# Reordering the opening of a fused attention and gMLP kernel: all x chunks ahead of the first weights, next x chunks behind all weights, and 1/std spread by small stationary products

## The chip, the cores and the metric

The kernel runs on one core of a Trainium2 chip. The metric is the device time of one launch in microseconds; lower is better. A "span" is the length of the profiled part of one run. It is 2.0 to 2.1 us less than the time of that run for the kernel before. Before the change the time was 796.73 us (median of 3 runs, 796.6 to 797.34). Three later sessions, on chips that the record numbers 0 (experiments 1 to 4), 6 (5 to 8) and 5 (9 to 12), each with its own runs of the kernel before, gave medians of 796.76, 797.1 and 796.79 us.

## The reference, cut to what matters

```python
x = A_x                                            # [1, 2048, 1024], bf16
h  = x + A(layernorm(x), wq, wk, wv, wo, beta)     # 4 segments of 512 tokens, 32 heads of 32:
                                                   # causal attention within the segment, mixed by a gate
                                                   # sigmoid(beta) with a linear memory of earlier segments
h2 = h + B(layernorm(h), w_in, w_sp, b_sp, w_out)  # gelu, spatial matmul [2048 x 2048], w_out
```

Only the opening matters here: the normalization of the first 512 tokens (segment 0, four chunks of 128 tokens), its projections q, k and v, and the first steps of attention. A step is one group of four heads; there are 32 of them.

## The kernel before

A recorder notes every operation and inserts the semaphores that its operands need; each engine gets its own list, and in the timelines below its instructions come in that order. All operations carry the line of that recorder (L209) in the profile, so groups are told apart by their tiles.

In segment 0 the division by the standard deviation is put off: only the mean is taken off x before the projections, and 1/std multiplies v, q and k when they are evicted from PSUM. For q and k, 1/std must lie along the columns, so it is spread over all partitions (tile `rb`) by TensorE. The loads, all on one queue:

```python
for k in range(8):                       # order: x0, x1, wv0, x2, wv1, x3, wv2, wv3
    if k in (0, 1, 3, 5): x_load((k + 1) // 2)             # 128 rows of x, 256 KB
    else: ... sp.dma_start(WV[0][:, i:i + 2, :], ...)      # a quarter of w_v's first half, 256 KB
sp.dma_start(WK[:, :, 0:256], ...)
sp.dma_start(BETAB[:], ...)
sp.dma_start(WQ[:, :, 0:256], ...)
sp.dma_start(WV[1][:], ...)
```

The opening:

```python
warm(9)                                  # nine dummy products, stationary IDENT
act_mean(1)                              # ScalarE: mean of chunk 1
var0(ln_stats(XCH[0]))                   # VectorE: bn_stats x2, bn_aggr of chunk 0
c0 = center(0, MV[0][:, 0:1], ALU.subtract)
c1 = center(1, MEAN[1][:])
pe_Th(0, c0, dve, dve)                   # 8 transposes on TensorE, evicted by VectorE
pe_Th(1, c1, act, dve)
...                                      # 8 v products, chunk 2, 8 v products, chunk 3 (cut)
proj_v(0, 2, 0)
gates()                                  # sigmoid(beta): ScalarE, then three ops on VectorE
mask_g()                                 # GpSimd: copy of GS (1024 columns), four multiplies
mm8(bank(bk), ... WK ...)                # k of step 0
for i in range(2): pe.matmul(bank(br), ONES[:], DIAG[i] ...)     # spread 1/std
act.activation(RB[:], bank(br), ACTF.Copy)
qk_out(0, 1, bk)                         # VectorE: evict k times RB
mm8(bank(bq), ... WQ ...)
qk_out(0, 0, bq)
for tc in range(4, 8): x_load(tc)        # segment 1
sp.dma_start(WK[:, :, 256:D], ...)       # the rests of w_k and w_q, 1.5 MB each
sp.dma_start(WQ[:, :, 256:D], ...)
phi_exp(0); phi_max(0)                   # phi_max starts with a bf16 add of 1.0 on VectorE (tile pqk)
```

In step 0, the k product of step 1 fills PSUM bank 6, and the q product of step 1 is later written to the same bank. The program lets TensorE start that q product only when VectorE has evicted the k product (`qk_out`).

The softmax here doesn't subtract the row's maximum and nothing guards it: scores larger than these inputs give would overflow.

## Time and profile before

| | before |
|---|---|
| time, median | 796.73 us |
| TensorE busy | 789.9 of 795.1 us |
| first transpose | 6.10 us |
| first w_k product | 14.04 us |
| first logits (step 0) | 19.75 us |

The page of the kernel before: the first line is each engine's busy time, the second the chain of work that ended last, as shares of the span. PE is TensorE, PEld its loading of stationary operands, DVE is VectorE, ACT ScalarE, POOL GpSimd, and SPq the queue of SyncE, which issues the loads.

```profile
PE 789.9 (99%) x5657; PEld 378.4 (48%) x5657; DVE 379.3 (48%) x745; ACT 295.6 (37%) x347; POOL 172.1 (22%) x329
...
PE 96%; DMA 2%; DVE 1%; ACT 0%; SPq 0%; issue 0%
```

TensorE is all there is to gain from, and it is nearly full. So the next view is TensorE's timeline in the opening: start in us, duration in us, engine, line, operation, out<-in, shapes, count, and in brackets the idle time before the group and what ended it. Among the tiles, `lno` is a chunk with its mean taken off, `xnT` its transpose, `qk` the evicted q and k, and `e` the exponentials of the logits.

```profile
1.74 4.02 PE L209 MATMUL ps<-etmp,ident 128*128 128x512 bf16 x9 [1.74 <-DVE ident L209]
6.10 1.14 PE L209 MATMUL ps<-ident,lno 128*128 128x128 bf16 x16 [0.34 <-DVE lno L209]
7.09 0.39 PE L209 MATMUL ps<-wv,xnT 128*128 128x512 bf16 x1
7.71 1.68 PE L209 MATMUL ps<-wv,xnT 128*128 128x512 bf16 x7 [0.23 <-ACT xnT L209]
...
14.04 1.89 PE L209 MATMUL ps<-xnT,wk 128*128 128x512 bf16 x8
15.76 0.59 PE L209 MATMUL ps<-diag,ones 128*128 128x512 bf16 x2
...
19.75 0.40 PE L209 MATMUL ps<-qk 32*128 32x512 bf16 x4
...
21.81 0.59 PE L209 MATMUL ps<-xnT,wq 128*128 128x512 bf16 x2
...
24.72 0.29 PE L209 MATMUL ps<-qk 32*128 32x256 bf16 x4 [0.15 <-ACT e L209]
```

A product of 512 columns shows as 0.38 us, but eight of them start 0.216 us apart (14.04 to 15.76), so their records overlap. Read starts, not durations: from 6.10 on the starts follow each other almost without holes. What lies before 6.10, plus a few tenths at 7.31, 9.22, 24.4 and 29.8, is all that a better opening can give; the prediction estimates it at about 2 us.

### The profile page before, as it was taken

The page shows a single profiled execution, that of the slowest core. Times are in us where ns is not written, and L with a number is a line of the kernel's source. Part 1 is how long each engine was busy: PE and PEld are TensorE (multiplying, and loading weights), DVE is VectorE, ACT ScalarE, POOL GpSimd, SP SyncE. Part 2 cuts the span into 40 slices and gives each one's busy share as a digit, 9 for nine tenths or more (in the row PEclk, how much of TensorE's full clock was granted, in tenths as well). Part 3 has the DMA queues.
Part 4 walks back from the last instruction along what each step waited for, and adds up shares of the span by engine and source line. Part 5 has one row for each costly group of instructions (what it writes and reads, how often), then busy time and mean ns, then how long its engine had stood idle before and what let it go on. Part 6 is the DMA issues. An engine that isn't in the chain of part 4 may idle for free.

```text
span 795.1 us, 13111 instructions
## 1 busy us (share of the span) xinstructions
PE 789.9 (99%) x5657; PEld 378.4 (48%) x5657; DVE 379.3 (48%) x745; ACT 295.6 (37%) x347; POOL 172.1 (22%) x329
## 2 busy tenths in 40 slices
PE   8999999999999999999999999999999999999998
PEld 3445455554554455455544444444444444444444
DVE  7664689679854766744562000053234323323332
ACT  5777877887787675133333333100000000000000
POOL 4564565565553331100230000000000000000000
DMA  9862555363415325411116000740270043011002
GB/s 292 181 162 57 94 81 121 87 105 84 107 23 125 114 67 139 121 47 54 54 54 132 1 1 0 222 90 7 79 133 1 33 109 78 1 59 54 1 7 86
DMA packets 125002, 64.83 MB, mean 82 GB/s; under 512 B 94992, under 2 KB 113936, under 8 KB 124944
## 3 DMA queue, kind: packets, MB, share of 16 engines
q1 hardware_dynamic: 124944, 63.99, 33.7%
q8 instruction: 44, 0.72, 0.4%
q14 instruction: 14, 0.11, 0.1%
HBM read 32.51 MB, written 8.39 MB: 51 GB/s over the span
## 4 chain that ended last, share of the span: by engine, by line
PE 96%; DMA 2%; DVE 1%; ACT 0%; SPq 0%; issue 0%
PE ps L209 96%; DMA wq<-in_A_wq_dram 2%; DMA xch<-in_A_x_dram 0%; DVE stats L209 0%; ACT junk L209 0%; DVE xnT L209 0%; DVE lno L209 0%; SPq L209 0%; ACT xnT L209 0%; DVE mv L209 0%; DVE fin L209 0%
## 5 line engine op out<-in xcount | busy, mean ns | idle before, releaser
L209 PE MATMUL ps<-wspT,z 128*128 128x512 bf16 x896 | 194.0, 379 | 0.0
L209 ACT ACTIVATE e<-ps 128x2048 bf16<-128x2048 f32 (+1 forms) x96 | 152.6, 1590 | 41.9 <-PE ps L209 41.8
L209 PEld LDWEIGHTS ps<-wspT,z 128*128 128x128 bf16 x896 | 87.7, 98 | 105.7
L209 DVE TENSOR_TENSOR tmpg<-ps,brow 128x512 f32<-128x512 f32 x56 | 38.7, 691 | 196.7 <-DMA brow<-in_B_b_sp_dram 104.0
L209 POOL TENSOR_SCALAR_AFFINE_SELECT e<-e 128x512 bf16<-128x512 bf16 x128 | 90.4, 718 | 127.2 <-ACT e L209 127.1
L209 PE MATMUL ps<-win,hnT 128*128 128x448 bf16 x512 | 98.3, 352 | 0.0
L209 PE MATMUL ps<-w_out,yT 128*128 128x512 bf16 (+2 forms) x462 | 97.4, 373 | 0.0
L209 PE MATMUL ps<-hnT,win 128*128 128x512 bf16 x448 | 96.9, 379 | 0.0
L209 PEld LDWEIGHTS ps<-win,hnT 128*128 128x128 bf16 x512 | 49.7, 98 | 46.4 <-issue 0.2
L209 PEld LDWEIGHTS ps<-w_out,yT 128*128 128x128 bf16 x462 | 44.7, 98 | 52.3
L209 PEld LDWEIGHTS ps<-hnT,win 128*128 128x128 bf16 x448 | 43.8, 98 | 52.8
L209 PE MATMUL ps<-xnT,wk 128*128 128x512 bf16 x256 | 60.8, 380 | 0.0
L209 PE MATMUL ps<-xnT,wq 128*128 128x512 bf16 x256 | 60.6, 379 | 0.1
L209 PE MATMUL ps<-wv,xnT 128*128 128x512 bf16 x256 | 59.4, 380 | 0.2 <-ACT xnT L209 0.2
L209 ACT ACTIVATE z<-ps 128x448 bf16<-128x448 f32 x60 | 32.5, 543 | 69.4 <-PE ps L209 69.4
L209 PE MATMUL ps<-wo,oT 128*128 128x512 bf16 x256 | 58.0, 379 | 0.0
L209 ACT ACTIVATE z1T<-ps 128x512 bf16<-128x512 f32 x56 | 33.4, 597 | 63.3 <-PE ps L209 63.3
L209 DVE TENSOR_TENSOR fin<-fin,ps 128x512 bf16<-128x512 bf16 (+2 forms) x33 | 22.2, 671 | 71.2 <-DMA fin<-out_dram 39.7
L209 DVE BATCH_NORM_STATS2 zst<-z 128x6 f32<-128x448 bf16 x64 | 38.9, 619 | 30.1 <-ACT z L209 30.1
L209 PEld LDWEIGHTS ps<-v,e 128*128 128x128 bf16 x1280 | 38.8, 96 | 14.0 <-issue 6.5
L209 PE MATMUL ps<-v,e 128*128 128x33 bf16 x1280 | 42.2, 178 | 0.0
L209 DVE TENSOR_TENSOR yT<-tmpg,z1T 128x512 bf16<-128x512 f32 x56 | 38.8, 692 | 1.9
(86 smaller groups left out, 609.3 us busy)
## 6 DMA issues: line engine op xcount, KB each, us to landing
xch<-in_A_x_dram SPq DMA_DIRECT2D x16, 256.0 KB, 3.3
xr<-in_A_x_dram SPq DMA_DIRECT2D x16, 256.0 KB, 3.7
out_dram<-hch SPq DMA_DIRECT2D x16, 256.0 KB, 2.4
fin<-out_dram SPq DMA_DIRECT2D x16, 256.0 KB, 2.8
out_dram<-fin SPq DMA_DIRECT2D x31, 128.0 KB, 1.7
win<-in_B_w_in_dram SPq DMA_DIRECT2D x4, 896.0 KB, 5.1
w_out<-in_B_w_out_dram SPq DMA_DIRECT2D x1, 3584.0 KB, 12.7
win<-in_B_w_in_dram SPq DMA_DIRECT2D x3, 1024.0 KB, 5.2
```

Source lines behind the costliest of these rows:

```text
L209: ins = getattr(e, op.name)(*op.args, **op.kw)
```

## The change

The intent is to start real work earlier and to take work off VectorE. All four x chunks go ahead of w_v. Chunk 0's mean is taken in halves by two engines. Variances are computed later. The 512-column products with `DIAG` become eight 128-column products whose stationary operand is a broadcast column of 1/std. The rests of w_k and w_q go ahead of segment 1's x chunks, whose normalization starts two steps later. Smaller shifts that go with this, in which engine evicts some v products and in the order within steps 0 to 2, are cut.

```diff
-    for k in range(8): ...                      # x0 x1 wv0 x2 wv1 x3 wv2 wv3
+    for tc in range(4):
+        x_load(tc)
+    for i in range(0, 8, 2):
+        sp.dma_start(WV[0][:, i:i + 2, :], ...)
 ...
     sp.dma_start(WV[1][:], wcols(A_wv, 512, D))
+    sp.dma_start(WK[:, :, 256:D], wcols(A_wk, 256, D))      # moved up
+    sp.dma_start(WQ[:, :, 256:D], wcols(A_wq, 256, D))
 ...
-            pe.matmul(bank(7), IDENT[:], ETMP[:, 0, :], start=True, stop=True)      # warm
+            pe.matmul(bank(7), ETMP[:, 0, 0:128], ETMP[:, 0, :], start=True, stop=True)
 ...
     warm(9)
+    act_half(0)                    # ScalarE sums columns 512..1023
+    dve_half(0)                    # VectorE sums columns 0..511, adds the two
+    center_half(0, 0)
+    center_half(0, 1)
+    pe_Th(0, LNO[0], dve, dve)
+    act_mean(1)
+    v_pair(0, 0, 2)                # first two v products: need the first w_v piece
+    c1 = center(1, MEAN[1][:])
+    pe_Th(1, c1, dve, dve)
+    v_pair(0, 2, 4)
 ...                                # chunks 2 and 3 between the other v products
+    stats0(0, 0) ... stats0(3, 1)  # variances of chunks 0 and 3 on VectorE, 1 and 2 on ScalarE
+    dve.tensor_copy(RSB[:, 0, :], RSW[:, :, 0])             # 1/std as two bf16 parts
+    dve.tensor_tensor(RSB[:, 1, :], RSW[:, :, 0], RSB[:, 0, :], ALU.subtract)
     proj_v(0, 2, 0)
     mm8(bank(bk), ... WK ...)
+    q_part(0, bq, 0, 4)
+    for t in range(4):
+        for h in range(2):
+            pe.matmul(PS[:, br, t * 128:(t + 1) * 128], RSB[:, h, t:t + 1].to_broadcast([128, 128]), IDENT[:], ...)
     act.activation(RB[:], bank(br), ACTF.Copy)
     qk_out(0, 1, bk)
+    q_part(0, bq, 4, 8)
     qk_out(0, 0, bq)
+    gates()                        # moved behind the q/k evictions
+    mask_g()
 ...
-            f2 = [("qmm", n + 1, bq, 2, 8), ("qout", n + 1, 0, bq), ("vmm", 0, 0, 1, bv, 0, 2)]
+            f2 = [("qmm", n + 1, bq, 2, 8), ("qout", n + 1, 0, bq), ("vmm", 0, 0, 1, bv, 0, 3)]
```

More of the change, by code (lines that the diff above doesn't have):

```diff
@@ L321, in bass_sequential_preLN__memory_aug_infini_attn__mixer_gmlp__prompt_kernel @@
     RDM = cb("rdm", [128, 4, 4], F32)
-    RS0 = [cb("rs0%d" % i, [128, 1], F32) for i in range(4)]
+    RSW = cb("rsw", [128, 4, 8], F32)
+    RS0 = [RSW[:, i, 0:1] for i in range(4)]
     HNT = [tens("hnT0", [128, 8, L], BF16, 14 * K), tens("hnT1", [128, 8, L], BF16, 22 * K),
@@ L338, in bass_sequential_preLN__memory_aug_infini_attn__mixer_gmlp__prompt_kernel @@
     b1 = Bump(110 * K, 120 * K)
-    ONES = b1("ones", [128, 128], BF16)
+    HSUM = b1("hsum", [128, 1], F32)
     MEAN = [b1("mean%d" % i, [128, 1], F32) for i in range(4)]
     RB = b1("rb", [128, L], F32)
-    DIAG = [b1("diag%d" % i, [128, 4, 128], BF16) for i in range(2)]
+    RSB = b1("rsb", [128, 2, 4], BF16)
     JUNK = b1("junk", [128, D], BF16)
@@ L398, in wcols @@
         return ap[:, lo:hi].rearrange("(c p) n -> p c n", p=128)
-    for k in range(8):
-        if k in (0, 1, 3, 5):
-            x_load((k + 1) // 2)
-        else:
-            i = {2: 0, 4: 2, 6: 4, 7: 6}[k]
-            sp.dma_start(WV[0][:, i:i + 2, :],
-                         A_wv[i * 128:(i + 2) * 128, 0:512].rearrange("(c p) n -> p c n", p=128))
+    for tc in range(4):
+        x_load(tc)
+    for i in range(0, 8, 2):
+        sp.dma_start(WV[0][:, i:i + 2, :], A_wv[i * 128:(i + 2) * 128, 0:512].rearrange("(c p) n -> p c n", p=128))
     sp.dma_start(WK[:, :, 0:256], wcols(A_wk, 0, 256))
@@ L410, in bass_sequential_preLN__memory_aug_infini_attn__mixer_gmlp__prompt_kernel @@
     sp.dma_start(WV[1][:], wcols(A_wv, 512, D))
+    sp.dma_start(WK[:, :, 256:D], wcols(A_wk, 256, D))
+    sp.dma_start(WQ[:, :, 256:D], wcols(A_wq, 256, D))
     pool.memset(MHALF[:], -0.5)
-    dve.memset(ETMP[:], 0.0)
+    dve.memset(ETMP[:, 0, :], 0.0)
     act.activation(RDM[:, 0, 0:1], MHALF[:], ACTF.Exp)
@@ L418, in bass_sequential_preLN__memory_aug_infini_attn__mixer_gmlp__prompt_kernel @@
     pool.memset(BLK[:], 1.0)
-    pool.memset(ONES[:], 1.0)
     pool.affine_select(out=BLK[:], in_=BLK[:], pattern=[[-32, 4]], compare_op=ALU.is_ge, fill=0.0, base=0,
@@ L482, in v_out @@
         v = bank(b).rearrange("p (h d) -> p h d", d=32)
-        if (s, tcl, half) == (0, 3, 0):
-            dve.tensor_single_scalar(o, v, RS0[tcl][:], ALU.mult)
+        if (s, tcl, half) in ((0, 3, 0), (0, 0, 1)):
+            dve.tensor_single_scalar(o, v, RS0[tcl], ALU.mult)
         else:
-            act.activation(o, v, ACTF.Copy, scale=RS0[tcl][:] if s == 0 else 1.0)
+            act.activation(o, v, ACTF.Copy, scale=RS0[tcl] if s == 0 else 1.0)
     def v_mm(s, tcl, half, b, i):
@@ L681, in rstd0, with act_half @@
     def rstd0(tc):
-        pool.tensor_tensor(RS0[tc][:], RS[tc][:, 0:1], MHALF[:], ALU.pow)
-    def diag(tc):
-        dve.tensor_single_scalar(DIAG[0][:, tc, :], IDENT[:], RS0[tc][:], ALU.mult)
-        dve.scalar_tensor_tensor(DIAG[1][:, tc, :], IDENT[:], RS0[tc][:], DIAG[0][:, tc, :], ALU.mult, ALU.subtract)
+        pool.tensor_tensor(RS0[tc], RS[tc][:, 0:1], MHALF[:], ALU.pow)
     def pe_Th(tcl, src, e0, e1):
         pe_T(XNT[0], tcl, src, (e0, e1))
-    warm(9)
+    def act_half(tc):
+        act.activation(JUNK[:, 512:D], XCH[tc][:, 512:D], ACTF.Copy, scale=-1.0 / D, accum_out=MEAN[tc][:])
@@ new lines, in dve_half, with center_half, stats0 @@
+    def dve_half(tc):
+        dve.tensor_reduce(out=HSUM[:], in_=XCH[tc][:, 0:512], axis=mybir.AxisListType.X, op=ALU.add)
+        dve.scalar_tensor_tensor(MEAN[tc][:], HSUM[:], -1.0 / D, MEAN[tc][:], ALU.mult, ALU.add)
+    def center_half(tc, h):
+        dve.tensor_single_scalar(LNO[tc % 3][:, h * 512:(h + 1) * 512], XCH[tc][:, h * 512:(h + 1) * 512],
+                                 MEAN[tc][:], ALU.add)
+    def stats0(k, i):
+        dve.bn_stats(STATS[k][:, i, :], XCH[k][:, i * 512:(i + 1) * 512])
@@ L692, in bass_sequential_preLN__memory_aug_infini_attn__mixer_gmlp__prompt_kernel, with aggr0, v_pair @@
+    def aggr0(k):
+        dve.bn_aggr(MV[k][:], STATS[k][:])
+        var0(k)
+        rstd0(k)
+    def v_pair(t, lo, hi):
+        for i in range(lo, hi):
+            v_mm(0, t, 0, vb[t], i)
+    warm(9)
+    act_half(0)
[3 more added lines that the diff above has]
+    pe_Th(0, LNO[0], dve, dve)
     act_mean(1)
-    var0(ln_stats(XCH[0]))
-    c0 = center(0, MV[0][:, 0:1], ALU.subtract)
+    vb = [next_bank() for _ in range(2)]
+    v_pair(0, 0, 2)
     c1 = center(1, MEAN[1][:])
-    pe_Th(0, c0, dve, dve)
@@ L697, in bass_sequential_preLN__memory_aug_infini_attn__mixer_gmlp__prompt_kernel @@
-    pe_Th(1, c1, act, dve)
+    pe_Th(1, c1, dve, dve)
+    v_pair(0, 2, 4)
     act_mean(2)
-    rstd0(0)
-    var0(ln_stats(XCH[1]))
-    rstd0(1)
+    v_pair(1, 0, 4)
+    v_pair(0, 4, 6)
     c2 = center(2, MEAN[2][:])
     act_mean(3)
-    vb = [next_bank() for _ in range(2)]
-    for i in range(4):
-        for t in range(2):
-            v_mm(0, t, 0, vb[t], i)
-    pe_Th(2, c2, act, dve)
-    c3 = center(3, MEAN[3][:])
-    for i in range(4, 8):
-        for t in range(2):
-            v_mm(0, t, 0, vb[t], i)
@@ L713, in bass_sequential_preLN__memory_aug_infini_attn__mixer_gmlp__prompt_kernel @@
-    var0(ln_stats(XCH[2]))
-    rstd0(2)
-    pe_Th(3, c3, act, dve)
-    act_var(3)
-    rstd0(3)
-    diag(0)
-    v_out(0, 0, 0, vb[0])
-    diag(1)
-    diag(2)
-    diag(3)
-    v_out(0, 1, 0, vb[1])
-    proj_v(0, 2, 0)
+    pe_Th(2, c2, dve, act)
+    v_pair(1, 4, 6)
+    v_pair(0, 6, 8)
+    v_pair(1, 6, 8)
+    c3 = center(3, MEAN[3][:])
+    stats0(0, 0)
+    act_var(1)
+    rstd0(1)
+    pe_Th(3, c3, dve, act)
+    stats0(0, 1)
+    aggr0(0)
+    act_var(2)
+    rstd0(2)
+    stats0(3, 0)
@@ new lines, in bass_sequential_preLN__memory_aug_infini_attn__mixer_gmlp__prompt_kernel @@
+    stats0(3, 1)
+    aggr0(3)
+    dve.tensor_copy(RSB[:, 0, :], RSW[:, :, 0])
+    dve.tensor_tensor(RSB[:, 1, :], RSW[:, :, 0], RSB[:, 0, :], ALU.subtract)
+    rot["n"] = 4
+    proj_v(0, 2, 0)
+    v_out(0, 1, 0, vb[1])
+    v_out(0, 0, 0, vb[0])
+    bq, br, bk = 5, 6, 7
+    mm8(bank(bk), lambda i: WK[:, i, 0:128], lambda i: XNT[0][:, i, :])
+    q_part(0, bq, 0, 4)
+    for t in range(4):
+        for h in range(2):
+            pe.matmul(PS[:, br, t * 128:(t + 1) * 128], RSB[:, h, t:t + 1].to_broadcast([128, 128]), IDENT[:],
+                      start=(h == 0), stop=(h == 1))
@@ L725, in bass_sequential_preLN__memory_aug_infini_attn__mixer_gmlp__prompt_kernel @@
+    act.activation(RB[:], bank(br), ACTF.Copy)
+    qk_out(0, 1, bk)
+    q_part(0, bq, 4, 8)
+    qk_out(0, 0, bq)
     gates()
     mask_g()
-    bk, bq, br = next_bank(), next_bank(), next_bank()
-    mm8(bank(bk), lambda i: WK[:, i, 0:128], lambda i: XNT[0][:, i, :])
-    for i in range(2):
-        pe.matmul(bank(br), ONES[:], DIAG[i][:].rearrange("p c n -> p (c n)"), start=(i == 0), stop=(i == 1))
-    act.activation(RB[:], bank(br), ACTF.Copy)
-    qk_out(0, 1, bk)
-    mm8(bank(bq), lambda i: WQ[:, i, 0:128], lambda i: XNT[0][:, i, :])
@@ L734, in bass_sequential_preLN__memory_aug_infini_attn__mixer_gmlp__prompt_kernel @@
-    qk_out(0, 0, bq)
     for tc in range(4, 8):
         x_load(tc)
-    sp.dma_start(WK[:, :, 256:D], wcols(A_wk, 256, D))
-    sp.dma_start(WQ[:, :, 256:D], wcols(A_wq, 256, D))
     phi_exp(0)
@@ L741, in bass_sequential_preLN__memory_aug_infini_attn__mixer_gmlp__prompt_kernel @@
     rot["banks"] = [6, 7]
+    rot["n"] = 0
     CH = [("z2", FH + 448 * k, 448) for k in range(4)] + [("z1", 512 * k, min(512, FH - 512 * k)) for k in range(4)]
@@ L808, in fill @@
                  "vmm": v_part, "vout": v_out}[u[0]](*u[1:])
-        if s < NSEG - 1 and c < 4:
-            ln_tasks(XCH[c], XNT[(s + 1) % 2], c)
+        if s < NSEG - 1 and 0 <= c - 2 * (s == 0) < 4:
+            t = c - 2 * (s == 0)
+            ln_tasks(XCH[t], XNT[(s + 1) % 2], t)
         if s < NSEG - 2 and c >= 4:
@@ L817, in bass_sequential_preLN__memory_aug_infini_attn__mixer_gmlp__prompt_kernel @@
         if n == 0:
-            fill(f1)
-            f1 = [("v", 0, 3, 0)]
             bq, bv = 6, 7
-            f1 += [("qmm", n + 1, bq, 0, 2)]
-            f2 = [("qmm", n + 1, bq, 2, 8), ("qout", n + 1, 0, bq), ("vmm", 0, 0, 1, bv, 0, 2)]
-            f3 = [("vmm", 0, 0, 1, bv, 2, 8), ("vout", 0, 0, 1, bv)]
+            fill([("qk", 1, 1)])
+            f1 = [("vmm", 0, 3, 0, bv, 0, 8), ("vout", 0, 3, 0, bv), ("qmm", n + 1, bq, 0, 2)]
+            f2 = [("qmm", n + 1, bq, 2, 8), ("qout", n + 1, 0, bq), ("vmm", 0, 0, 1, bv, 0, 3)]
+            f3 = [("vmm", 0, 0, 1, bv, 3, 8), ("vout", 0, 0, 1, bv)]
         logits(n, 0)
@@ L830, in bass_sequential_preLN__memory_aug_infini_attn__mixer_gmlp__prompt_kernel @@
             pv(n - 1, (3,))
-        bg_pop()
+        if n != 2:
+            bg_pop()
         fill(f2)
+        if n == 2:
+            bg_pop()
         logits(n, 2)
@@ L843, in bass_sequential_preLN__memory_aug_infini_attn__mixer_gmlp__prompt_kernel @@
         bg_pop()
+        if n == 0:
+            rot["n"] = 0
         if n == 1:
```

## The prediction

Gains of 0.8, 0.2 and 0.1 us make 1.1, and less the 0.5 given back they make 0.6, so 796.1 from 796.73 us. The landing expected for w_v rests on the eight landings that the text lists.

> **What bounds the kernel.** TensorE. The engine table gives PE 789.9 of 795.1 us (99%), the chain of waits is 96% PE. A 512-column matmul group of eight takes 1.73 us start to start in the timeline (0.216 us each). Only the opening can give anything: the change leaves nearly everything from step 3 on alone and swaps two 512-column products for eight 128-column ones (sixteen 128-column transposes take 1.14 us: no difference).
>
> **What the opening holds** (PE timeline, 0 to 35 us). Warm-up products 1.74 to 5.76; first transpose at 6.10; then gaps inside the first v products (7.31 to 7.71 and 9.22 to 9.68), w_k products at 14.04, first logits at 19.75, and about 0.3 us at 24.72 waiting for ACT to read the logits banks. After 6.10 all holes together are about 1.2 us; the chain before 6.10 is x chunk 0 landing at 3.83, two bn_stats (1.41), aggregate (0.21), centring (0.49). So at most some 2 us, a quarter of a per cent, is to be had.
>
> **Gains.**
> 1. Mean of chunk 0 by halves: ACT half about 0.55 + 0.19 us, DVE half beside it about 0.6, a tiny add, then half a centring 0.25. First transpose near 5.2 to 5.4 in place of 6.10: minus 0.8 us. Warm-up starts about 0.4 us earlier (half the memset, no identity).
> 2. bn_stats and the diag building (2.4 us of DVE) leave the path of the transposes.
> 3. A third v product ahead of the third logits covers the wait at 24.72: minus 0.2 us.
> 4. w_k/w_q rests no longer queue behind chunks 4 to 7 or behind the read of chunk 3 (14.0 us): w_q lands at about 22 to 24 us in place of 30.07. But PE waited only 0.2 us for it, so minus 0.1 at most.
>
> **Costs.** The first w_v piece, third on the queue before, landed at 6.1 us (issue 1.71 plus 4.4); it is now fifth. By position the landings of before were 3.83, 4.45, 6.1, 7.4, 8.1, 8.8, 9.6, 10.35 us, so I expect it at 7.3 to 8, and PE, done with chunk 0's transposes by 5.9, idles about 1.5 us. This gives back most of gain 1. [...] First w_k product: 13.5 to 14.1 against 14.04. Pool's mask (5.6 us) starts later; small risk for the first pv products.
>
> **Sum.** Gains 1.1, minus 0.5 given back: about 0.6 us. Predicted 796.1 us, 8 in 10 between 794.7 and 797.4. Chances: faster by over 2% 0.0, within 2% 0.995, slower 0.005.
>
> **What shows it.** Right: first transpose before 5.5 us; first w_v landing after 7 us with a PE wait for DMA of wv of 1 us or more (before: none); w_q rest landed before 25; no ACT wait of 0.3 us at the third logits; first logits between 19.2 and 19.9. Wrong: w_v landing by 6.3, or first logits much before 19.
>
> **What would make it wrong.** A PE clock that falls back to half rate in the new idle gap (warm-up products take 0.43 us each, later ones 0.216); [...] Pool's later mask holding up pv; DVE, which now carries more evictions, pacing chunks 1 to 3.

## The result, and the profile after

The time after is 797.31 us (median of 6 runs, 797.02 to 798.95), beside 796.68 us of the kernel before (6 runs). The ratio is 1.0009 with a 95% interval of 0.9996 to 1.0022. Ratios in this text are the mean time of one kernel's fast runs over that of the other's of the same rounds, so they are not quite the ratios of the quoted medians. One of the six runs, the one at 798.95 us, had a mean granted TensorE clock of 0.998 where all others had 1.0.

The page of the kernel after, the same two lines. The count of PE is lower only because the trace lacks some matmul records: PEld has six more, as the change asks (eight small products for two large ones).

```profile
PE 784.8 (99%) x5571; PEld 378.5 (48%) x5663; DVE 378.7 (48%) x741; ACT 296.6 (37%) x349; POOL 166.9 (21%) x328
...
PE 95%; DVE 3%; issue 1%; DMA 1%; SPq 0%; ACT 0%
```

TensorE's timeline of the kernel after, in the same columns:

```profile
1.24 4.02 PE L209 MATMUL ps<-etmp 128*128 128x512 bf16 x9 [1.24 <-DVE etmp L209]
5.06 0.73 PE L209 MATMUL ps<-ident,lno 128*128 128x128 bf16 x8
7.58 0.59 PE L209 MATMUL ps<-wv,xnT 128*128 128x512 bf16 x2 [1.79 <-DMA wv<-in_A_wv_dram]
...
14.13 1.89 PE L209 MATMUL ps<-xnT,wk 128*128 128x512 bf16 x8
15.86 1.03 PE L209 MATMUL ps<-xnT,wq 128*128 128x512 bf16 x4
16.92 0.62 PE L209 MATMUL ps<-ident,rsb 128*128 128x128 bf16 x8
...
20.07 0.40 PE L209 MATMUL ps<-qk 32*128 32x512 bf16 x4
...
22.71 0.60 PE L209 MATMUL ps<-xnT,wq 128*128 128x512 bf16 x2 [0.41 <-DVE qk L209]
...
25.63 0.29 PE L209 MATMUL ps<-qk 32*128 32x256 bf16 x4
```

Four things are to be seen. Real work starts a microsecond earlier (5.06), but the first v product waits 1.79 us for w_v, and the first w_k product is not earlier at all (14.13 against 14.04). Four products of w_q start at 15.86 and need 0.86 us, yet the spreading products start at 16.92, 0.2 us after the last of them could have ended: they waited for `rsb`. And there is a new hole before 22.71, for an eviction of VectorE. Against that, the wait for ScalarE before the third logits is gone.

The hole at 22.71 is explained by VectorE's timeline. This is the kernel before, from the eviction of q of step 0 to the eviction of k of step 1:

```profile
18.12 0.69 DVE L209 TENSOR_TENSOR qk<-ps,rb 128x512 bf16<-128x512 f32 x1 [0.41 <-PE ps L209]
18.73 0.28 DVE L209 TENSOR_SCALAR pqk<-qk 128x512 bf16<-128x512 bf16 x1
...
19.85 0.69 DVE L209 TENSOR_TENSOR qk<-ps,rb 128x512 bf16<-128x512 f32 x1
```

The same view of the kernel after:

```profile
19.41 0.17 DVE L209 TENSOR_SCALAR gs<-gs 128x32 f32<-128x32 f32 x1
...
20.10 1.13 DVE L209 TENSOR_SCALAR pqk<-qk 128x512 bf16<-128x512 bf16 x1
...
21.97 0.68 DVE L209 TENSOR_TENSOR qk<-ps,rb 128x512 bf16<-128x512 f32 x1
```

GpSimd's timeline of the kernel after, at the same moment:

```profile
20.04 1.05 POOL L209 COPY maskg<-gs 128x1024 f32<-128x1024 f32 x1 [3.57 <-DVE gs L209]
```

The gate arithmetic now stands between the evictions (0.7 us), and the add behind it takes 1.13 us in place of 0.28 (20.10 to 21.23), about as long as GpSimd's copy runs (1.05 us, 20.04 to 21.09). Counted from the first logits, the eviction starts 1.90 us later (21.97 minus 20.07) in place of 0.10 us (19.85 minus 19.75), and TensorE's eight v products cover only about 2 us.

### The profile page after: what moved, and what is told of

The parts are those of the page before. It is cut to its first block, busy times and chain, and to the rows that moved or that the text cites. A ratio compares the mean times of both kernels' runs of the same rounds, so it can differ in the third digit from the quotient of the medians.

```text
span 795.4 us, 13031 instructions
## 1 busy us (share of the span) xinstructions
PE 784.8 (99%) x5571; PEld 378.5 (48%) x5663; DVE 378.7 (48%) x741; ACT 296.6 (37%) x349; POOL 166.9 (21%) x328
## 4 chain that ended last, share of the span: by engine, by line
PE 95%; DVE 3%; issue 1%; DMA 1%; SPq 0%; ACT 0%
PE ps L209 95%; DVE stats L209 1%; DMA wv<-in_A_wv_dram 1%; DVE pqk L209 0%; DVE hch L209 0%; DVE otok L209 0%; DVE qk L209 0%; SPq L209 0%; DVE ta L209 0%; DVE lno L209 0%; DVE rd L209 0%; DVE etmp L209 0%; DVE rdm L209 0%; ACT rb L209 0%; DVE gs L209 0%
## 5 line engine op out<-in xcount | busy, mean ns | idle before, releaser
L209 PE MATMUL ps<-xnT,wq 128*128 128x512 bf16 x226 | 54.3, 379 | 2.1 <-DVE qk L209 0.4
```

Of the source, the lines that this page charges most:

```text
L209: ins = getattr(e, op.name)(*op.args, **op.kw)
```

## The experiments

All twelve were correct. The times of the kernel after come from an earlier session than those of the experiments.

### 1. The old load order in the kernel after

```diff
-    for tc in range(4): x_load(tc)
-    for i in range(0, 8, 2): sp.dma_start(WV[0][:, i:i + 2, :], ...)
+    # x0, x1, wv0, x2, wv1, x3, wv2, wv3, as in the kernel before
```

> The kernel after, with only the load order of before put back (x0, x1, w_v piece 0, x2, w_v 1, x3, w_v 2, w_v 3). Theory (position on the queue): the first w_v piece lands about 1.3 us earlier (near 6.1 us in place of 7.44), TensorE's wait of 1.8 us for w_v falls under 0.6 us, and the last piece still lands near 9.7, so the first w_k product starts at 13.4 to 13.9 in place of 14.13 and the time falls by 0.2 to 0.7 us against the kernel after. Rival (the w_v transfers are slow by themselves, whatever stands ahead of them, or the eviction chain on VectorE paces the opening): the wait for w_v only changes its name, the first w_k product stays within 0.1 us of 14.13 and the time doesn't move.

Its one profile fell into a run of 1016.4 us at a granted clock of 0.753. That is a different state of the chip and says nothing here. The four fast runs took 796.26 to 796.79 us, all at clock 1.0. It was run again as experiment 5.

### 2. Gates and mask early

```diff
+    gates()
+    mask_g()
     bq, br, bk = 5, 6, 7
     mm8(bank(bk), ... WK ...)
 ...
     qk_out(0, 0, bq)
-    gates()
-    mask_g()
```

> The kernel after, with the gate arithmetic and the mask's building recorded ahead of the first w_k product, where the kernel before has them. Theory (new wait in step 0 comes from the late gates): the mask's copy on GpSimd then ends before VectorE's first bf16 add of 1.0, which takes 0.28 us again in place of 1.13; the q/k eviction that stood at 21.97 us comes to about 20.2, and TensorE's hole before the two w_q products (22.29 to 22.71, 0.41 us by the waits) goes. Steps after it start 0.4 to 0.6 us earlier than in the kernel after, and the time falls by 0.3 to 0.6 us. Rival (the hole is TensorE's own, or the eviction is late because RB is late): the hole stays above 0.3 us and the time does not move.

TensorE's timeline of this kernel in step 0:

```profile
22.68 0.39 PE L209 MATMUL ps<-qk 32*128 32x512 bf16 x4
...
24.74 0.59 PE L209 MATMUL ps<-xnT,wq 128*128 128x512 bf16 x2
```

The hole is gone. From first logits to the w_q products it takes 2.06 us in place of 2.64 (22.71 minus 20.07), as in the kernel before (2.06). Over the following steps the 0.59 us are kept: the first logits of step 1 come 6.39 us after those of step 0 (29.07), in place of 6.98 (27.05 in the kernel after). The theory held. The add took 0.52 us, not the expected 0.28.

The three runs at clock 1.0 took 796.58 to 797.0 us, where the five such runs of the kernel after took 797.02 to 797.71 in their earlier session, about what 0.59 us promises. Two runs, however, took 798.13 and 799.16 us at a mean clock of 0.998, so that the median is 797.0. The profile is of the longest and shows why it was long; the other was not profiled. The view is busy time by stretch: from and to in us, length, then busy time (and count) of PE, PEld, DVE, ACT, POOL, the granted clock, the DMA share and GB/s.

```profile
9.00:9.50 0.50, 0.50 (x10) 0.50 (x9) 0.10 (x1) 0.00 (x0) 0.00 (x0) 0.84 1.14 353
9.50:10.00 0.50, 0.50 (x4) 0.22 (x3) 0.50 (x2) 0.00 (x0) 0.00 (x0) 0.50 1.19 316
...
12.50:13.00 0.50, 0.50 (x6) 0.28 (x5) 0.00 (x0) 0.00 (x0) 0.00 (x0) 0.75 0.78 258
```

The timeline of TensorE in the same run:

```profile
8.54 0.59 PE L209 MATMUL ps<-wv,xnT 128*128 128x512 bf16 x2 [2.45 <-DMA wv<-in_A_wv_dram]
...
9.48 3.51 PE L209 MATMUL ps<-wv,xnT 128*128 128x512 bf16 x8
```

In this run w_v landed a microsecond later than in the profile of the kernel after (its first product starts at 8.54 in place of 7.58), TensorE idled for 2.45 us, and its clock stood at half rate for about 3.4 us (from 9.34, where a stretch with a mean of 0.84 puts the step, to 12.75). Eight products took 3.51 us in place of 1.9. Half of 3.4 us lost is 1.7 us, which is 0.002 of the span: a mean granted clock of 0.998, as listed for this run.

### 3. The mask's copy in eight pieces

```diff
-        pool.tensor_copy(MASKG[:, :, :, 0:32], GS[:]...to_broadcast([128, NQ, 4, 32]))
+        for c in range(NQ):
+            pool.tensor_copy(MASKG[:, c, :, 0:32], GS[:, 4 * c:4 * c + 4].unsqueeze(2).to_broadcast([128, 4, 32]))
```

> The kernel after, with the mask's one GpSimd copy of 1024 columns (1.05 us) made as eight copies of 128 columns; nothing moves in the program's order. Two readings of the late eviction: (a) VectorE's add of 1.0 (1.13 us beside 0.28 in the kernel before) was held by the GpSimd copy that ran at the same time, for as long as that one instruction ran; then the add falls to 0.3 to 0.6 us and the eviction after it starts about 0.6 us earlier, TensorE's hole shrinks under 0.15 us, time minus 0.2 to 0.5. (b) the add is slow for another reason, and the eviction is late because the gate arithmetic (0.8 us) stands ahead of it on VectorE: then the add stays at 1.0 us or more and nothing moves.

VectorE's timeline of this kernel, its add of 1.0:

```profile
20.09 0.39 DVE L209 TENSOR_SCALAR pqk<-qk 128x512 bf16<-128x512 bf16 x1
```

TensorE's timeline of this kernel: the first logits and w_q products of step 0, and the products of probabilities and v in step 1:

```profile
20.06 0.40 PE L209 MATMUL ps<-qk 32*128 32x512 bf16 x4
...
22.12 0.59 PE L209 MATMUL ps<-xnT,wq 128*128 128x512 bf16 x2
...
30.05 0.27 PE L209 MATMUL ps<-v,e 128*128 128x33 bf16 x4 [0.88 <-POOL e L209]
```

Reading (a) held: with the same program order the add fell from 1.13 to 0.39 us, and the w_q products started 2.06 us after the first logits. So the copy held VectorE up. The time did not fall (797.54 to 800.68 us, median 797.93; against the kernel before the ratio is 1.0024, 1.0012 to 1.0036), because eight small copies take GpSimd 2.81 us in place of 1.05, its masking of the probabilities comes later (first at 27.22 us in place of 25.57), and TensorE waits 0.88 us for it. More than the gain was given back one step later, on another engine: from the first logits of step 0 to the third of step 1 it takes 12.75 us (20.06 to 32.81) in place of 12.29 (20.07 to 32.36).

### 4. Chunk 0's statistics early

```diff
     c1 = center(1, MEAN[1][:])
+    stats0(0, 0); stats0(0, 1); aggr0(0)
     pe_Th(1, c1, dve, dve)
 ...                                        # and removed from their place near chunk 3
```

> The kernel after, with the variance statistics of chunk 0 on VectorE moved up to the idle stretch after the centring of chunk 1 (6.76 to 8.43 us). Theory: the spread of 1/std waits for chunk 3's statistics, which stand behind chunk 0's on VectorE; with those out of the way the bf16 copy of 1/std comes at about 15.6 in place of 16.50 us, TensorE's hole of 0.3 to 0.4 us before the spreading products (LDWEIGHTS at 16.92) goes, first logits at 19.6 to 19.8 in place of 20.07. As the later wait in step 0 hangs on the same evictions, everything after moves by the same 0.3 to 0.4 us, and the time falls by as much. Rival (1/std is paced by ScalarE's two squared sums and GpSimd's powers): copy of 1/std within 0.3 us of 16.5, no gain.

TensorE's timeline of this kernel, the spreading products and the first logits:

```profile
16.67 0.61 PE L209 MATMUL ps<-ident,rsb 128*128 128x128 bf16 x8
...
19.80 0.39 PE L209 MATMUL ps<-qk 32*128 32x512 bf16 x4
```

The hole before the spreading products went, and first logits came at 19.80 in place of 20.07, a little less than the expected gain. From first w_k to first logits it took 5.72 us (14.08 to 19.80) in place of 5.94. The copy of 1/std came at 16.18, later than the 15.6 expected: behind the statistics the powers on GpSimd (the last ends at 16.15) and the sums on ScalarE (GpSimd waits for one of them for 0.91 us, until 14.37) are nearly as late. The times were 796.88 to 800.18 us (median 797.89; ratio to the kernel before 1.0017, 1.0006 to 1.0029), again with long runs that hide the 0.27 us.

### 5. The old load order once more

> The same kernel as in the first experiment (the kernel after with the load order of before), because its only profile fell into a run of 1016 us at a granted clock of 0.75. Expected as then: first w_v piece at about 6 us, no single wait for w_v above 0.6 us, first w_k product at 13.4 to 13.9, first logits 0.2 to 0.6 us earlier than the 20.07 of the kernel after, and no run with a granted clock of 0.998 and 1.5 to 3 us more, as there were in 5 of the 23 runs with all x chunks first. Rival (those runs have nothing to do with the order of the loads): one or two of these five are such runs too.

TensorE's timeline of this kernel, where it waits for w_v:

```profile
6.02 0.59 PE L209 MATMUL ps<-wv,xnT 128*128 128x512 bf16 x2 [0.44 <-DMA wv<-in_A_wv_dram]
...
8.10 2.10 PE L209 MATMUL ps<-wv,xnT 128*128 128x512 bf16 x8 [0.88 <-DMA wv<-in_A_wv_dram]
```

The one wait of 1.79 us became two of 0.44 and 0.88 us, so the theory is right about the first piece and was too hopeful about the second. First w_k came at 13.95 us and first logits at 19.88, where the kernel after has 14.13 and 20.07. The product came a little later than the 13.4 to 13.9 expected. The five times were 796.28 to 796.96 us, median 796.41, all at clock 1.0; that does not separate it from the kernel before of the same session (ratio 0.9994, 0.9981 to 1.0007).

### 6. Only the load order, in the kernel before

```diff
-    for k in range(8): ...                # x0 x1 wv0 x2 wv1 x3 wv2 wv3
+    for tc in range(4): x_load(tc)        # then the four w_v pieces
```

> The kernel before, with only the order of the first eight loads taken from the change (all four x chunks first). Theory: TensorE there starts its transposes at 6.1 and has those of two chunks to do before it needs w_v, so the late piece (7.44) costs only about 0.3 us of wait; the rest of the opening is paced as before: first w_k product within 0.3 us of 13.8, time within 0.4 us of the kernel before, and the gap stays too short for a fall of the clock. Rival (the x-first order is bad by itself): wait above 0.8 us, time 0.5 us or more slower, runs at 0.998.

TensorE's timeline of this kernel, its wait for w_v and the first w_k product:

```profile
7.61 1.89 PE L209 MATMUL ps<-wv,xnT 128*128 128x512 bf16 x8 [0.62 <-DMA wv<-in_A_wv_dram]
...
13.79 1.89 PE L209 MATMUL ps<-xnT,wk 128*128 128x512 bf16 x8
```

The wait was 0.62 us, more than the 0.3 expected and less than the rival's 0.8. The times, 796.57 to 797.27 us, don't differ from those of the kernel before of the same session (796.43 to 797.43), and no run had a lower clock. The order by itself is therefore nearly harmless where TensorE has two chunks to transpose first. It hurts in the new schedule, which asks for w_v after one chunk.

### 7. Only the weights first, in the kernel before

```diff
     sp.dma_start(WV[1][:], ...)
+    sp.dma_start(WK[:, :, 256:D], ...); sp.dma_start(WQ[:, :, 256:D], ...)   # moved up
 ...
-        if s < NSEG - 1 and c < 4:
-            ln_tasks(XCH[c], XNT[(s + 1) % 2], c)
+        if s < NSEG - 1 and 0 <= c - 2 * (s == 0) < 4:                       # two steps later in segment 0
+            t = c - 2 * (s == 0)
+            ln_tasks(XCH[t], XNT[(s + 1) % 2], t)
```

The edit also shifts one background task in step 2, as the change does (cut here).

> The kernel before, with only the rests of w_k and w_q issued ahead of x chunks 4 to 7, and with the shift by two steps of the next segment's normalization that goes with it. Theory: w_q lands near 25 to 26 us in place of 30.07, and TensorE's hole of about 0.28 us at 29.83 to 30.11 goes; VectorE has no statistics of the next segment in step 0, so the other waits of step 0 stay or shrink; time 0.2 to 0.5 us less than before. Rival (w_q was never what TensorE waited for): the w_q products of step 1 start within 0.1 us of where they did, no gain.

TensorE's timeline of this kernel, the first logits of step 0 and the third of step 1:

```profile
19.25 0.39 PE L209 MATMUL ps<-qk 32*128 32x512 bf16 x4
...
31.16 0.29 PE L209 MATMUL ps<-qk 32*128 32x256 bf16 x4
```

The rival held. From the first logits of step 0 to the third logits of step 1 it took 11.91 us (19.25 to 31.16), exactly as in the second profile of the unchanged kernel (19.34 to 31.25, experiment 12). Only the first profile has 12.19 us there (19.75 to 31.94), with the hole at w_q; there w_q landed at 30.07 us, in the second profile at 28.2, before it was needed (29.43). The median of 796.37 us against 797.1 looks like a gain, but both kernels' spans go from 794.3 to about 795.2, and the ratio is 0.9997 (0.9983 to 1.0010).

### 8. All three repairs

The edits of experiments 1, 2 and 4 together.

> The kernel after with three things at once: load order of before, gate arithmetic and mask ahead of the first w_k product, chunk 0's statistics in VectorE's idle stretch. If the three causes add: about 0.5 (w_v wait) + 0.55 (hole in step 0) + 0.26 (hole before the spreading) less than the kernel after's 795.4 us span, that is a span of about 794.1 and a time of about 795.8 us, roughly 0.9 us below the kernel before. If they overlap (one wait only hands over to the next), less than 0.6 us below the kernel after.

TensorE's timeline of this kernel, its longest wait:

```profile
8.88 1.47 PE L209 MATMUL ps<-wv,xnT 128*128 128x512 bf16 x6 [0.81 <-DVE xnT L209]
```

The time was 795.99 to 796.36 us, median 796.31, half a microsecond short of the hoped-for 795.8 (ratio to the kernel before 0.9990, 0.9978 to 1.0003). The causes overlap: with w_v early, the statistics that experiment 4 had put into VectorE's idle stretch stood in front of the eviction of chunk 1, and the wait for w_v became a wait of 0.81 us for that eviction. First w_k stayed at 14.11. The idle stretch had been a product of the late load.

### 9. A longer gap on purpose

```diff
     for tc in range(4): x_load(tc)
+    sp.dma_start(WK[:, :, 0:256], ...)    # 512 KB, moved ahead of w_v
     for i in range(0, 8, 2): ...
```

> The kernel after, with the first w_k piece (512 KB) put ahead of the w_v pieces, so that TensorE's idle gap after chunk 0's transposes grows from 1.8 us to about 3 to 3.5 us on purpose. Theory (an idle gap of this length makes the clock fall, as in the one profile with a granted clock of 0.70 between 7.4 and 13 us, gap 2.5 us): now most or all of the runs, not one in five, show a mean granted clock of 0.998 and about 1.7 us more than the gap itself costs; time 799.5 to 801.5 us; in the profile the v products after the gap take 0.427 us each for about 3.4 us. Rival (the fall of the clock has nothing to do with the gap): clock 1.0 in nearly all runs, time 798 to 799 us.

### 10. The same gap, filled

```diff
+    warm(14)
     v_pair(0, 0, 2)
```

> The kernel of the last experiment with 14 dummy products (zeros, as in the warm-up, about 0.216 us each at full clock, 3.0 us together) between chunk 0's transposes and the first v product. Theory: the loads land as late as there, but TensorE is not idle, so the granted clock stays 1.0 in all runs and the time is 1.5 to 2 us below the long gap's. Rival (the late loads alone make the runs slow): same time as the long gap within 0.5 us.

TensorE's timeline with the gap empty (experiment 9):

```profile
9.74 1.01 PE L209 MATMUL ps<-wv,xnT 128*128 128x512 bf16 x2 [4.12 <-DMA wv<-in_A_wv_dram]
```

The granted clock in the same run, by stretch as in experiment 2:

```profile
8.00:8.50 0.50, 0.00 (x0) 0.00 (x0) 0.00 (x0) 0.50 (x2) 0.00 (x0) 0.87 1.10 349
...
15.00:15.50 0.50, 0.50 (x10) 0.50 (x8) 0.07 (x1) 0.00 (x0) 0.00 (x0) 0.80 1.09 350
```

TensorE's timeline with the gap filled (experiment 10):

```profile
5.81 3.19 PE L209 MATMUL ps<-etmp 128*128 128x512 bf16 x14
10.01 0.59 PE L209 MATMUL ps<-wv,xnT 128*128 128x512 bf16 x2 [1.01 <-DMA wv<-in_A_wv_dram]
```

The gap became 4.12 us, longer than meant. All five runs had a clock of 0.996 and took 801.64 to 802.38 us. The profile has the clock at half from about 8.4 to 15.2 us; it fell 2.8 us into the gap. The loss is more than was expected: the half rate lasted twice as long as in experiment 2 (6.8 us against 3.4). With dummy products in the gap all five runs had 1.0 and took 799.08 to 799.61 us, although there the first v product could start only at 10.01, against 9.74. The medians differ by 2.45 us, more than the 1.5 to 2 expected. An estimate from the profiles gives as much: half of the work time at half rate (9.74 to 15.2) is 2.7 us, less 0.27 for the later start. The two programs differ in nothing but the dummy products, so in this pair it is TensorE's idleness (a gap of 4.12 us against one of 1.01) that drops the clock.

### 11. The repairs, with chunk 0's statistics out of the way

```diff
     pe_Th(1, c1, dve, dve)
+    stats0(0, 0)
 ...
     c2 = center(2, MEAN[2][:])
+    stats0(0, 1); aggr0(0)
```

with the old load order and the early gates of experiments 1 and 2.

> The kernel with all three repairs, but with chunk 0's statistics behind chunk 1's eviction (first half) and behind chunk 2's centring (second half), not ahead of chunk 1's eviction, where they made TensorE wait 0.81 us for the eviction of chunk 1. Expected: that wait falls under 0.3 us, the first w_k product starts at 13.4 to 13.8 in place of 14.11, everything after moves by 0.3 to 0.6 us, the granted clock is 1.0 in all runs, time 795.5 to 796.0 us. Rival (the w_v loads pace the opening whatever VectorE does): the wait moves to w_v, gain under 0.2 us.

TensorE's timeline of this kernel, its two waits in the opening:

```profile
6.04 0.60 PE L209 MATMUL ps<-wv,xnT 128*128 128x512 bf16 x2 [0.26 <-DVE xnT L209]
...
8.07 2.07 PE L209 MATMUL ps<-wv,xnT 128*128 128x512 bf16 x8 [0.68 <-DMA wv<-in_A_wv_dram]
```

The time is 795.62 to 796.11 us, median 795.81; the nine runs of the kernel before in the same session took 796.52 to 797.28. The ratio is 0.9988 (0.9975 to 1.0000), and no run of one kernel lies within the range of the other, so this version beats the kernel before by about 1 us. The kernel after was not run beside it; its median, from earlier runs, is 1.5 us higher. Of the 1 us, 0.35 lie outside the span, as with every kernel of the new opening; the mean spans differ by 0.63 us (794.10 against 794.73). The wait for the eviction fell to 0.26 us, but 0.68 us of it moved to the second w_v piece, and the first w_k product came at 13.89, later than expected; so the rival is right in part. This profile is of the longest of its runs (span 794.4; the others 793.9 to 794.1), and its marks (first logits at 19.61, third logits of step 1 at 31.32) are no earlier than those of experiment 12 (19.34 and 31.25). Where the shorter runs gain their further 0.3 to 0.5 us is therefore not shown.

### 12. The kernel before again

> The kernel before, unchanged, for a second profile. Its runs fall into two groups of span, 794.3 to 794.5 and 795.0 to 795.4 us, and the profile that the prediction was made from belongs to the slower one. Theory: the groups differ in when x chunk 0 lands (3.83 us there; 3.4 in the two variants of it whose profiles belong to the faster group). If this profile is of the faster group: first transpose at 5.65 to 5.75 in place of 6.10, first w_k product at about 13.55, and no wait for w_q. If of the slower: landing near 3.83 and first transpose near 6.1 again. Rival: a fast span with the late landing, or the other way round.

TensorE's timeline of this second profile of the unchanged kernel, at the marks used before:

```profile
5.77 1.07 PE L209 MATMUL ps<-ident,lno 128*128 128x128 bf16 x16 [0.46 <-DVE lno L209]
...
13.64 1.89 PE L209 MATMUL ps<-xnT,wk 128*128 128x512 bf16 x8
...
19.34 0.40 PE L209 MATMUL ps<-qk 32*128 32x512 bf16 x4
```

x chunk 0 landed at 3.51 us here in place of 3.83, and the span was 794.4 us, in the faster part of the range. The profile that the prediction had used was of a run with late loads. That the two groups of spans are nothing but the landing of chunk 0 is not shown: in this last session the runs lie in between as well (794.5 to 795.2).

## Why the prediction was right or wrong

The measured 797.31 us lies within the predicted range of 794.7 to 797.4, and "within 2%" was right. The direction was not: 0.6 us less was forecast, and the medians show 0.6 us more, which the interval of the ratio does not separate from nothing. That the range held is in part luck: the median lies 0.09 us inside its upper end, two of the six runs (797.71 and 798.95) lie outside, and the errors below were covered by the width of the range. Of the prediction's own signs, two failed: first logits at 20.07 us and not between 19.2 and 19.9, and the rest of w_q landed after 25. Set against the second profile of the kernel before, whose loads came as early as those of the kernel after, the marks on TensorE are these (us):

| mark | before (12) | after | difference |
|---|---|---|---|
| first transpose | 5.77 | 5.06 | -0.71 |
| first w_k product | 13.64 | 14.13 | +0.49 |
| first logits, step 0 | 19.34 | 20.07 | +0.73 |
| second logits, step 0 | 21.93 | 23.25 | +1.32 |
| third logits, step 1 | 31.25 | 32.36 | +1.11 |
| span | 794.4 | 795.4 | +1.0 |

- **Bound.** Right. TensorE stays full from the third step on (after the third logits of step 1 it is busy for 760.82 of 763.16 us in the kernel before), and everything is decided before 32 us: what follows the third logits of step 1 takes 763.1 us before and 763.0 after.
- **Gain 1, the earlier start.** The mechanism was right: 5.06 us, ahead of the 5.2 to 5.4 given. Its size was taken from one profile with a late chunk 0. Against the second profile it is 0.7 us, not the 1.04 that the first two profiles show.
- **Cost, the late w_v.** Right in kind and nearly in size: landing at 7.44 (issue 2.65 plus 4.79) where 7.3 to 8 was expected, and a wait of 1.79 us where 1.5 was. The landings again follow the position on the queue: 3.4, 4.1, 5.8 and 6.8 us for the x chunks, then 7.44, 8.1 and 8.9 for the first three w_v pieces. But "gives back most of gain 1" was too mild. It gives back more than all of it: the first w_k product comes 0.49 us later, so 1.2 us are given back where the sum entered 0.5. The wait alone does this: from 7.58 us on TensorE has no hole, as 24 v products of 0.216 us and three sets of transposes of 0.44 make 6.5 of the 6.55 us to the first w_k product. Experiment 5 takes back 0.18 of the 0.49 us (13.95); two waits for w_v, of 0.44 and 0.88 us, remain there, because the new schedule asks for w_v after one chunk.
- **Gain 2, VectorE's work off the path.** This is the first step whose mechanism failed: the prediction looked only at what left VectorE. Diag building went, but the statistics of chunks 0 and 3 came in its place on the way to `rsb`, and that made a new wait: from first w_k to first logits it takes 5.94 us in place of 5.70. Experiment 4 took it away (5.72).
- **Missing term: the gates in the evictions' way.** The prediction saw the later mask only as a risk to the products with v. It cost elsewhere: +0.59 us between first and second logits (+0.73 to +1.32). Experiment 2 removes it by order, experiment 3 by cutting the copy, so the hold by GpSimd is a part of the cause and not a story: the add takes 1.13 us beside a copy of 1.05, and 0.39 beside pieces of it. Why the two engines hold each other up is not shown, nor what decides which of them waits. In the kernel before, the add and a GpSimd multiply start together at 18.73 us; the add took 0.28 us and the multiply 1.21, where the one ahead of it took 0.95, so there it seems to be GpSimd that waited. In experiment 2 the add (22.04 to 22.56) ran within a multiply (21.94 to 23.01): it took 0.52 us and did not wait for its end. Spans on GpSimd are rough. Experiment 3 then shows that the feared wait for GpSimd by the products with v exists too.
- **Gain 3, the third v product.** Right: the wait for ScalarE before the third logits is gone, and the difference falls by 0.21 us between the second logits and step 1.
- **Gain 4, w_q earlier.** The rest landed at 25.7 us (11.43 plus 14.3), not at 22 to 24 (the author's estimate, whose working the record does not give), and nothing was gained: experiment 7 shows no difference to the unchanged kernel's second profile. The 0.28 us hole was seen in the first profile only.
- **The named risk of the clock came true in some runs.** Experiments 2, 9 and 10 show the fall and its cause here. A gap of 2.45 us was followed by half rate for 3.4 us, beginning 0.8 us after work had resumed (experiment 2); in a gap of 4.12 us the clock fell 2.8 us into the gap and stayed at half for 6.8 us (experiment 9). What length of gap is needed is not shown. Of the 23 fast runs of the kernel after and of experiments 2 to 4 (x first), 5 had a mean clock of 0.998. Of the 19 fast runs of its schedule with the old order (experiments 1, 5, 8, 11) none had, and none took over 797.0 us. The groups were run in different sessions, in part on different chips (on chip 0 alone 4 of 17 against none of 4), so that the load order sets how often this happens is likely, not shown. If so, the kernel after is also less even than its schedule with the old order. In the profile of the kernel after, with its gap of 1.79 us, the clock did not fall. The first v product, which waits for the fifth load on the queue, started between 7.33 and 8.54 us in the four profiles with x first (kernel after, experiments 2 to 4); the clock fell in the one that started at 8.54 and in none of the other three, and the other runs at 0.998 have no profile. The warm-up products that the prediction took as a sign of a half rate do start 0.43 us apart, twice the later 0.216, but the profile's granted clock is 1.00 between 1.0 and 5.2 us of the kernel after: it does not show the slow start.

Left open: four other runs of experiments 3 and 4 had a span 0.6 to 3.3 us above the shortest of their kernel at a clock of 1.0. They were not profiled; late loads would explain them, but that is not shown.

## What to carry to other kernels

Here x chunks 2 and 3 moved forward on a shared queue moved the first w_v piece back (landing at 7.44 us, against 6.1 in the first profile of the kernel before and 5.1 in the second): ask first what the engine that bounds the kernel will have to do in the meantime, and whether the gap is long enough to cost it its clock, as gaps of 2.45 and 4.12 us did and one of 1.79 did not. Work put "off the path" must be checked against what it now stands in front of, in its own engine's list and on the other engines that it can hold up (VectorE's add: 1.13 us beside GpSimd's copy, 0.28 in the kernel before); experiments 3 and 8 each removed one wait only to make another. For tenths of a microsecond, one profile is not a baseline: take two, and compare starts of the same products rather than totals.
